# Second layer of batches 2 to 4 in block products with its output transposed, all weights made during batch 1

## The chip, the cores and the metric

The kernel runs on one core of a Trainium2 chip. The metric is the device time of one execution in microseconds; before the change the median of three runs is 2445.89 (2444.21 to 2447.18). The engines are PE (matrix products), DVE (vector), ACT (scalar activation), POOL (the general engine) and SP (here it issues the DMAs). Each engine works through its own instructions in a fixed order and stops where one of them has to wait.

## What is computed

Masked attention over four batches of eight heads, and a mixture of eight experts on its result, in which every token goes through every expert:

```python
    mask = q_assign[:, :, :, None] == k_assign[:, :, None, :]
    scores = np.where(mask, scale * np.matmul(q, k.transpose(0, 1, 3, 2)), -1000000000.0)
    ...
    for e in range(E):
        h = np.maximum(x @ w1[e], 0.0)
        ye = h @ w2[e]
        out += P[:, e:e + 1] * ye
```

x is 3072 x 512 (four batches of 768 tokens), w1 is 8 x 512 x 1024, w2 is 8 x 1024 x 512, all float32. P comes from eight rounds of normalising rows and columns (`gates`). Each operand of a product is held as two float16 numbers, a high part and the remainder, and each product is three matmuls: high by high, high by low, low by high.

## The kernel before

The attention takes the first 530 us. A planner orders its instructions by costs and due times written in the code; it also starts the first weight loads. The change touches one line of it: `largest` (line 290), the largest absolute value of a batch's x, is taken there for the first two batches.

Then come the experts. For every batch, expert and quarter f2 of the hidden size (256 of 1024) there is one step, 128 in all. In a step, layer 1 (`layer1`, with `product`, line 1219) forms four blocks of the hidden values by seven block products in place of eight, from sums of blocks of x (T1 to T4, made once a batch) and of blocks of w1 (S1 to S4, made for each weight). A product is six matmuls of 384 columns; PSUM tiles h_ps (two buffers) receive them, ACT takes m1 and c11 out (line 1252), DVE adds up u2, u3, c22, c21 and c12 (line 1247). ACT writes the high part hh of each block (line 1232), DVE the low part hl (line 1235). Layer 2 (`layer2`, lines 1287 to 1289) multiplies hh and hl as the stationary operand with wb, which holds w2 as high and low part: six token tiles, each six matmuls of 512 columns, into six PSUM tiles o_ps that collect over the four steps of an expert. DVE multiplies by the gate and adds to acc (`gated`, line 1307). The seven products of a step alternate with the six tiles of the step before it.

Batches are taken in pairs, (1, 2) and then (3, 4), and a pair goes through an expert before the next one begins. While the first pair runs, `make_w` makes the 32 weights, one in every two steps in the main: scale the raw weight (ACT, lines 1092 and 1103), four sums of w1 blocks (POOL, line 1101), high parts (ACT) and low parts (POOL, lines 1107, 1110, 1115). They are kept for the pair's first batch, stored to memory (`store_w`) and loaded again (`load_w`) for the others. `scan` loads every raw weight once more ahead of that, to find the largest value of an expert, which sets its scale. `next_x` prepares the x of a later batch. `plan.keep_order` at the end of each seventh of a step fixes the order of everything written so far.

## Time and profile before

| | |
|---|---|
| median of three runs | 2445.89 us |
| span of the profiled execution | 2448.7 us |
| attention, up to the first expert matmul | 532.4 us |
| experts, first matmul to last | 532.4 to 2444.3 us |
| DMA, mean over the span | 131 GB/s |

The profile page holds the span, the busy time of each engine, the chain of work that ended last and the costliest groups of instructions. A row of the timeline begins with start and duration in microseconds, then engine, line, operation, the tiles written and read, and in square brackets the idle time ahead of it and what ended it. A row of the groups ends with total busy time, the mean of one in nanoseconds, and the idle time ahead of the group. PE rows count pipelined matmuls: the distance between starts, and not the duration, is what one costs. PEld is the load of the stationary operand.

### The profile page before, as it was taken

The numbers are of one execution on the slowest core, as the hardware profiler recorded it, in microseconds if no ns is written. First come the engines' busy times: TensorE is split into PE (matmuls) and PEld (weight loads), VectorE is DVE, ScalarE is ACT, GpSimd is POOL, SyncE is SP. The second block draws the span as 40 slices with busy tenths as digits, with TensorE's granted clock in tenths as the row PEclk, the third lists the DMA queues.
The fourth block names the chain that finished last, engine by engine and source line by source line (L and its number), as shares of the span: only waits on it lengthen the run. The fifth ranks groups of instructions, "written<-read, shape, count | busy, mean of one in ns | idle before, by whom it ended". The sixth has DMA issues, their size and how long they took to land.

```text
span 2448.7 us, 32683 instructions
## 1 busy us (share of the span) xinstructions
PE 2383.3 (97%) x12848; PEld 1275.6 (52%) x12848; DVE 1342.4 (55%) x2354; ACT 836.1 (34%) x1616; POOL 672.4 (27%) x712
## 2 busy tenths in 40 slices
...
GB/s 145 119 101 121 102 150 152 84 125 155 164 220 218 146 196 133 212 142 186 171 156 129 127 135 145 95 113 99 95 95 96 111 102 95 95 95 109 104 104 90
DMA packets 154681, 320.29 MB, mean 131 GB/s; under 512 B 61088, under 2 KB 90528, under 8 KB 154016
## 3 DMA queue, kind: packets, MB, share of 16 engines
...
q14 instruction: 52, 0.43, 0.1%
...
## 4 chain that ended last, share of the span: by engine, by line
PE 86%; DVE 7%; issue 3%; ACT 2%; DMA 1%; POOL 0%; SPq 0%; POOLq 0%; ACTq 0%; DVEq 0%
PE h_ps L1219 34%; PE o_ps L1289 13%; PE o_ps L1287 13%; PE o_ps L1288 13%; PE av_ps L824 4%; PE max_ps L697 3%; PE exp_ps L765 2%; DVE mrt L701 2%; PE exp_ps L766 2%; DVE vsum L507 1%; PE misc_ps L557 1%; DVE hl L1235 1%; PE misc_ps L861 0%; ACT pe L772 0%; PE misc_ps L940 0%
## 5 line engine op out<-in xcount | busy, mean ns | idle before, releaser
L1219 PEld LDWEIGHTS <-wa 128*128 128x128 f16 x5376 | 528.1, 98 | 451.7 <-issue 26.9
L1219 PE MATMUL h_ps<-xsT,wa 128*128 128x384 f16 x3072 | 585.1, 327 | 9.2 <-DVE csum L1055 7.8
L1289 PE MATMUL o_ps<-wb,hl 128*128 128x512 f16 x1536 | 583.2, 380 | 1.4 <-DVE hl L1235 1.4
L1232 ACT ACTIVATE hh<-c 128x384 f16<-128x384 f32 x512 | 267.5, 523 | 927.7 <-DVE c L1247 916.6
L1288 PE MATMUL o_ps<-wb,hh 128*128 128x512 f16 x1536 | 583.1, 380 | 0.0
L1287 PE MATMUL o_ps<-wb,hh 128*128 128x512 f16 x1536 | 583.0, 380 | 0.0
L1235 DVE SCALAR_TENSOR_TENSOR hl<-c,hh 128x384 f16<-128x384 f32 x512 | 291.0, 568 | 493.1 <-ACT hh L1232 492.6
L1219 PE MATMUL h_ps<-xsB,wa 128*128 128x384 f16 x2304 | 421.4, 328 | 7.4 <-DVE c L1247 7.4
L1247 DVE SCALAR_TENSOR_TENSOR c<-h_ps,u 128x384 f32<-128x384 f32 x256 | 142.2, 555 | 193.1 <-PE h_ps L1219 193.0
L1289 PEld LDWEIGHTS <-hl 128*128 128x128 f16 x1536 | 150.5, 98 | 184.6 <-DVE hl L1235 3.4
L1247 DVE SCALAR_TENSOR_TENSOR u<-h_ps,m 128x384 f32<-128x384 f32 x256 | 142.3, 556 | 182.6 <-PE h_ps L1219 182.5
L791 POOL TENSOR_TENSOR psum<-psum,pe 128x512 f32<-128x512 f32 (+1 forms) x207 | 227.2, 1115 | 54.2 <-ACT pe L772 46.6
L1287 PEld LDWEIGHTS <-hh 128*128 128x128 f16 x1536 | 151.0, 98 | 139.2 <-issue 0.6
L1288 PEld LDWEIGHTS <-hh 128*128 128x128 f16 x1536 | 150.4, 98 | 139.6 <-issue 0.6
L701 DVE TENSOR_REDUCE mrt<-max_ps 128x1 f32<-128x512 f32 (+1 forms) x288 | 190.5, 683 | 46.3 <-PE max_ps L697 44.6
L1252 ACT ACTIVATE c<-h_ps 128x384 f32<-128x384 f32 x128 | 62.7, 490 | 424.7 <-PE h_ps L1219 424.7
L772 ACT ACTIVATE pe<-exp_ps 128x512 f32<-128x512 f32 x288 | 166.5, 597 | 88.8 <-PE exp_ps L766 82.6
L1101 POOL TENSOR_TENSOR r<-r 128x256 f32<-128x256 f32 x124 | 88.3, 733 | 372.4 <-ACT r L1092 370.0
L1307 DVE SCALAR_TENSOR_TENSOR acc<-o_ps,gates,acc 128x512 f32<-128x512 f32 x168 | 125.4, 747 | 41.3 <-PE o_ps L1289 41.1
L824 PE MATMUL av_ps<-pe,vn 128*64 128x512 f32 (+1 forms) x768 | 138.5, 504 | 0.0
L697 PE MATMUL max_ps<-kX,qX 96*128 96x256 f32 (+1 forms) x384 | 126.9, 393 | 5.5 <-DVE mrt L701 2.6
L766 PE MATMUL exp_ps<-qX,kX 98*128 98x512 f32 (+1 forms) x384 | 128.5, 347 | 0.0
...
## 6 DMA issues: line engine op xcount, KB each, us to landing
...
```

The costliest lines, as they stand in the source:

```text
L697: nc.tensor.matmul(ps[:, y * (z - a) : (y + 1) * (z - a)], t["qa"][0:96, i * P : (i + 1) * P], t["k2"][0:96, a:z], start=True, stop=True)
L701: nc.vector.tensor_reduce(out=t["mr"][:, i0 : i0 + ni, ni - 1], in_=ps.rearrange("p (x c) -> p x c", x=ni), axis=AX, op=ALU.max)
L766: nc.tensor.matmul(o, t["k2"][0:98, ki], t["qa"][0:98, a:z], start=False, stop=True)
L791: (nc.gpsimd if e == POOL else nc.vector).tensor_tensor(out=st[:, a:z], in0=old[a], in1=part, op=ALU.add)
L824: nc.tensor.matmul(av[o, a:z], vn[:, i, :], heads[t]["pe", c][:, i - i0], start=(i == 0), stop=False, skip_group_check=True)
L1219: nc.tensor.matmul(ps[:, 0:HB], wa[:, w_, a, c, :], x[:, x_, c, :], start=(first and s_ == 0), stop=(s_ == len(steps) - 1), skip_group_che ...
L1232: nc.scalar.activation(hh[:, 2 - i, o], src, AF.Relu)
L1235: nc.vector.scalar_tensor_tensor(out=hl[:, 2 - i, o], in0=src, scalar=0.0, in1=hh[:, 2 - i, o], op0=ALU.max, op1=ALU.subtract)
L1247: nc.vector.scalar_tensor_tensor(out=t, in0=ps[:, 0:HB], scalar=KAPPA, in1=x, op0=ALU.mult, op1=ALU.add)
L1287: nc.tensor.matmul(po[i], hh[:, t, ti], wbh[:, t], start=(first and t == 0), stop=False)
L1288: nc.tensor.matmul(po[i], hh[:, t, ti], wbl[:, t], start=False, stop=False)
L1289: nc.tensor.matmul(po[i], hl[:, t, ti], wbh[:, t], start=False, stop=(last and t == 1))
```

## The change

The first batch alone now runs through all eight experts and makes every weight (phase 1, 32 steps). Raw weights are loaded once, six steps ahead, into seven tiles; the largest values are taken from these tiles (`scan`). One weight is made in each step, with two additions: `second_matrix` makes the low part of wb on DVE in place of POOL, and `second_sums` forms four sums of w2 blocks (POOL) with their high (ACT) and low parts (DVE), tile w2s. Its own layer 2 is as before.

Batches 2 to 4 follow (phase 2) in 24 slots of batch and expert, 28 steps each. A step holds one product of layer 1 of this slot and one group of six matmuls of layer 2 of the slot before, all of 384 columns. Layer 2 now has seven block products too (`layer2b`): a stored block of w2 or of its sums (w2o) is stationary, the hidden blocks ho are moving, so the output comes out transposed. The hidden blocks stay in float32 (B11 to B22) and their differences T1 to T4 are formed by `minus`, on POOL but for T1 and T2 of the second half (g = 1), which are DVE's; `high` (ACT) and `low` (DVE) split them. The gate, now a row over tokens, is multiplied and added on POOL (`gated_block`); at the last expert `deliver` turns the block back by six transposes of PE and stores it. x of the next batch is prepared by `next_x` in the first batch and in the second slot of a batch, stored, and loaded again (`reload_x`). The attention takes `largest` for the first batch only.

```diff
-            if b < 2:
+            if b == 0:
...
-    order = [(2 * c + j, e) for c in range(B // 2) for e in range(E) for j in range(2)]
...
-    def begin(idx):
-
-        e, j = divmod(idx, NP2)
-        return j - 1 if e == 0 else 2 * NP2 + j - 1 if e == 1 else 2 * NP2 * e + 2 * j - NP2 - 1
-
-    made = {}
-    begins = {begin(i): i for i in range(NI)}
-    scan_at = {1: NP2 - 1, 2: 2 * NP2 - 1, **{e: 2 * NP2 * (e - 1) - NP2 - 1 for e in range(3, E)}}
...
-            if b == 0:
-                store_w(idx, wt)
-            if t in begins:
-                i = begins[t]
-                made[i] = w_tiles(True)
-                making = make_w(i, made[i])
-                if i + 1 < NI:
-                    load_raw(i + 1)
-            for x, t0 in scan_at.items():
-                if t0 == t:
-                    scanning = scan(x)
...
+        def second_matrix(idx, wb):
+            e = idx // NP2
+            r2 = raws[idx][:, 1024:2048].rearrange("p (j m) -> p j m", j=2)
+            nc.scalar.activation(wb[:, 0], r2, AF.Copy, scale=s2[:, e : e + 1])
+            nc.vector.scalar_tensor_tensor(out=wb[:, 1], in0=r2, scalar=s2[:, e : e + 1], in1=wb[:, 0], op0=ALU.mult, op1=ALU.subtract)
+
+        def second_sums(idx):
+            e = idx // NP2
+            r2 = raws[idx][:, 1024:2048].rearrange("p (j m) -> p j m", j=2)
+            S_ = sump.tile([P, 4, HD], F32, name="s2w")
+            sums(S_, r2[:, 1, 0:HD], r2[:, 0, 0:HD], r2[:, 1, HD:DO], r2[:, 0, HD:DO], nc.gpsimd)
+            yield
+            t = w2s[idx] = w2p.tile([P, 4, 2, HD], F16, name="w2s")
+            nc.scalar.activation(t[:, :, 0], S_, AF.Copy, scale=s2[:, e : e + 1])
+            nc.vector.scalar_tensor_tensor(out=t[:, :, 1], in0=S_, scalar=s2[:, e : e + 1], in1=t[:, :, 0], op0=ALU.mult, op1=ALU.subtract)
+            yield
...
+        def make_w(idx, wt):
+
+            e = idx // NP2
+            wa, wb = wt
+            raw, A, S_ = first_matrix(idx)
+            nc.scalar.activation(raw, raw, AF.Copy, scale=s1[:, e : e + 1])
+            sums(S_, A[:, 1, 0], A[:, 1, 1], A[:, 0, 0], A[:, 0, 1], nc.gpsimd)
+            yield
+            for o, a in ((A22, A[:, 0, 1]), (slice(A11, A12 + 1), A[:, 1])):
+                nc.scalar.copy(wa[:, 0, o], a)
+                nc.gpsimd.tensor_tensor(out=wa[:, 1, o], in0=a, in1=wa[:, 0, o], op=ALU.subtract)
+            yield
+            nc.scalar.copy(wa[:, 0, 3:7], S_)
+            nc.gpsimd.tensor_tensor(out=wa[:, 1, 3:7], in0=S_, in1=wa[:, 0, 3:7], op=ALU.subtract)
+            yield
+            second_matrix(idx, wb)
+            yield
+            yield from second_sums(idx)
...
+        def store_sums(idx):
+            e, f2 = divmod(idx, NP2)
+            nc.sync.dma_start(out=w2d[e][:, 3:7, f2], in_=w2s.pop(idx))
...
+        scans = {1: (4, 5), 2: (6, 7), **{i - 5: (i,) for i in range(8, NI)}}
...
+        for t in range(NI):
...
+            if t + AHEAD < NI:
+                load_raw(t + AHEAD)
+            if t + 1 < NI:
+                wts[t + 1] = w_tiles()
+                making = chain(making, make_w(t + 1, wts[t + 1]))
...
+            if t in scans:
+                scanning = chain(*(scan(i) for i in scans[t]))
+            if t == 8:
+                inputs = next_x(1)
...
+            for m, _ in enumerate(layer1(wt[0], xs[0], out_tile, keep)):
                 if m in (0, 1, 3, 4):
                     step(sink)
-                if m in (((6,), (0, 3, 6), ANY, ANY)[t - NP2 + 1] if NP2 - 1 <= t < 2 * NP2 - 1 else (0, 2, 3, 5) if t < 11 else (0, 3)):
+                if m in ANY:
                     step(scanning)
...
                 step(before)
                 step(making)
+                if m == 1:
+                    store_w(t, wt)
+                    store_sums(t)
+                if t == NI - 1:
+                    reload_x(1, RIGHT[m])
                 plan.keep_order()
...
+    slots = [(b, e) for b in range(1, B) for e in range(E)]
...
+    def minus(n, g, o, a, c, into, by):
+        d = blocks[n, g]
+        t = d[into] if into else hbp.tile([P, 2, HB], F32, name="T3", bufs=2)
+        by.tensor_tensor(out=t, in0=d[a], in1=d[c], op=ALU.subtract)
+        d[o] = t
+
+    def high(n, g, o):
+        t = halves_[n, g, o] = hop.tile([P, 2, 2, HB], F16, name="ho")
+        nc.scalar.copy(t[:, 0], blocks[n, g][o])
+
+    def low(n, g, o):
+        t = halves_[n, g, o]
+        nc.vector.tensor_tensor(out=t[:, 1], in0=blocks[n, g][o], in1=t[:, 0], op=ALU.subtract)
...
+    def plan_slot(n):
+
+        base = SLOT * (n + 1)
+        for g, (t3, t1, t2, t4), off in ((0, (-13, -12, -4, 4), -6), (1, (1, 2, 3, 5), -4)):
+            at(base + t3, minus, n, g, "T3", "B22", "B12", None, nc.gpsimd)
+            at(base + t1, minus, n, g, "T1", "B12", "B11", "B12", nc.vector if g else nc.gpsimd)
+            at(base + t2, minus, n, g, "T2", "B22", "T1", "B11", nc.vector if g else nc.gpsimd)
+            at(base + t4, minus, n, g, "T4", "B21", "T2", "B21", nc.gpsimd)
+            for i, (_, o) in enumerate(ORDER2):
+                at(base + 4 * i + off, high, n, g, o)
+                at(base + 4 * i + off + 1, low, n, g, o)
+        for i in range(7):
+            at(base + 4 * i - 8, load_left, n, i)
+        at(base - 8, load_gate, n)
...
+                for d in range(2):
+                    nc.tensor.transpose(
+                        out=ps[:, ((q - q0) * 2 + d) * P : ((q - q0) * 2 + d + 1) * P], in_=y[:, d, q * P : (q + 1) * P], identity=ident
+                    )
...
+            nc.gpsimd.tensor_tensor(out=a, in0=y, in1=G_, op=ALU.mult)
+            return
+        nc.gpsimd.tensor_tensor(out=y, in0=y, in1=G_, op=ALU.mult)
+        to = y if e == E - 1 else a
+        nc.gpsimd.tensor_tensor(out=to, in0=y, in1=a, op=ALU.add)
+        if e == E - 1:
+            at(time, deliver, n, r, j, y)
...
+    def layer2b(n):
+
+        base = SLOT * (n + 1)
+        pa, pb, pc, y = {}, {}, {}, {}
...
+        for i, (a, o) in enumerate(ORDER2):
+            for d in range(2):
+                ps, pl, name, first = ((pa, ps_a, "pa", i == 0), (pb, ps_b, "pb", i == 2), (pc, ps_c, "pc", i == 4))[(0, 0, 1, 1, 2, 1, 2)[i]]
+                if first:
+                    ps[d] = pl.tile([P, 512], F32, name=name)
+                ps = ps[d]
+                for g in range(2):
...
+                    for s_, (w_, h_, f) in enumerate(steps):
+                        nc.tensor.matmul(
+                            ps[:, 0:HB],
+                            w[:, 2 * g + f, w_, d * P : (d + 1) * P],
+                            h[:, h_, f],
+                            start=(first and g == 0 and s_ == 0),
+                            stop=(g == 1 and s_ == len(steps) - 1),
...
+                    if g == 1:
+                        if i in (1, 4, 5, 6) and d == 0:
+                            y[i] = yp.tile([P, 2, HB], F32, name="y")
+                        if i == 0:
+                            nc.scalar.copy(mt[:, d], ps[:, 0:HB])
+                        elif i == 1:
+                            nc.scalar.copy(y[i][:, d], ps[:, 0:HB])
+                        elif i == 2:
+                            plus(u2[:, d], mt[:, d], ps)
+                        elif i == 3:
+                            plus(u3[:, d], mt[:, d], ps)
+                        else:
+                            plus(y[i][:, d], (u3, mt, u2)[i - 4][:, d], ps)
+                        if d == 1 and i in (1, 4, 5, 6):
+                            r, j = {1: (0, 0), 4: (1, 1), 5: (1, 0), 6: (0, 1)}[i]
+                            gated_block(n, r, j, y[i], base + {1: 11, 4: 22, 5: 25, 6: SLOT + 9}[i])
+                    yield
...
+            def keep(name, c):
+                if name == "B11":
+                    nc.scalar.activation(out_tile(name), c[:, 0:HB], AF.Relu, scale=KAPPA)
+                else:
+                    rests.append(lambda: nc.scalar.activation(c, c, AF.Relu))
+
+            for m, _ in enumerate(layer1(wa, xs[b], out_tile, keep)):
+                if e == E - 1 and f2 == NP2 - 1 and b + 1 < B:
+                    reload_x(b + 1, RIGHT[m])
+                yield
+
...
+    for n in range(NS + 1):
+        one = layer1b(n) if n < NS else iter(())
+        two = layer2b(n - 1) if n else iter(())
+        if n < NS:
+            b, e = slots[n]
+            if e == 1 and b + 1 < B:
+                inputs = next_x(b + 1)
+            if e == E - 1 and b + 1 < B:
+                inputs = spread_gates(b + 1)
+        for s in range(SLOT):
...
+            step(one)
+            for f in old:
+                f()
+            for f, a in tasks.pop(now, ()):
+                f(*a)
+            if s % 7 == 5:
+                step(inputs)
+            step(two)
+            plan.keep_order()
```

The first place is ACT in the middle of the weight making. Before, a step that makes a weight holds these rows (r1 and r2 are the raw halves, c11 and the others the blocks of the hidden values):

```order
L1092 ACTIVATE r1_13106<-r1_13106,s1_96 128x1024 [waits DMAHW6_49]
L1103 ACTIVATE r2_13108<-r2_13108,s2_97 128x1024 [waits DMAHW7_49]
L1252 ACTIVATE c11_13398<-h_ps_13356 128x384 [waits PE_49,Activation_49]
L1232 ACTIVATE hh_13354<-c11_13398 128x384 [waits Activation_49]
L1106 CAST wa_13348<-r1_13106 128x256
L1106 CAST wa_13348<-r1_13106 128x512
L1109 CAST wa_13348<-r1_13106 128x1024 [waits Pool_49]
L1232 ACTIVATE hh_13354<-c22_13435 128x384 [waits DVE_49]
L1232 ACTIVATE hh_13354<-c21_13451 128x384 [waits DVE_49]
L1232 ACTIVATE hh_13354<-c12_13467 128x384 [waits DVE_49]
L1114 CAST wb_13349<-r2_13108 128x1024
L1252 ACTIVATE m1_13486<-h_ps_13479 128x384 [waits PE_49]
```

After, these rows of phase 1 run from the second-layer sums of one weight to those of the next (raw is the raw weight, c the blocks):

```order
L1238 ACTIVATE w2s_8111<-s2w_8089,s2_97 128x4x256 [waits DMAHW6_49,Pool_49]
L1373 ACTIVATE hh_7988<-c_8120 128x384 [waits DVE_49]
L1147 ACTIVATE m1_8140<-h_ps_8133 128x384 [waits PE_49]
L1268 ACTIVATE raw_7384<-raw_7384,s1_96 128x1024
L1272 CAST wa_8129<-raw_7384 128x256 [waits DMAHW2_49,Activation_49]
L1272 CAST wa_8129<-raw_7384 128x512
L1370 ACTIVATE c_8187<-h_ps_8133 128x384 [waits PE_49]
L1373 ACTIVATE hh_8131<-c_8187 128x384 [waits Activation_49]
L1275 CAST wa_8129<-s1w_8150 128x1024 [waits Pool_49]
L1228 ACTIVATE wb_8130<-raw_7384,s2_97 128x1024 [waits DMAHW5_49,DMAHW4_49,DMAHW3_49]
L1373 ACTIVATE hh_8131<-c_8225 128x384 [waits DVE_49]
L1373 ACTIVATE hh_8131<-c_8247 128x384 [waits DVE_49]
```

The high part w2s of the sums, which waits for POOL, stands ahead of the last hh of the step, of m1 and of the scaling of the next raw weight.

The second place is POOL in the same two stretches. Before, one weight is:

```order
L1101 TENSOR_TENSOR r1_11089<-r1_11089 128x256 [waits DMAHW2_49,Activation_49]
L1101 TENSOR_TENSOR r1_11089<-r1_11089 128x256 [waits Pool_49]
L1101 TENSOR_TENSOR r1_11089<-r1_11089 128x256
L1101 TENSOR_TENSOR r1_11089<-r1_11089 128x256 [waits Pool_49]
L1107 TENSOR_TENSOR wa_11343<-r1_11089,wa_11343 128x256 [waits DMAHW6_49,PE_49,Activation_49]
L1107 TENSOR_TENSOR wa_11343<-r1_11089,wa_11343 128x512 [waits Activation_49]
L1110 TENSOR_TENSOR wa_11343<-r1_11089,wa_11343 128x1024 [waits Activation_49]
L1115 TENSOR_TENSOR wb_11344<-r2_11091,wb_11344 128x1024 [waits DMAHW7_49,PE_49,Activation_49]
```

After, one weight is:

```order
L1219 TENSOR_TENSOR s1w_8150<-raw_7384 128x256 [waits DMAHW7_49,Activation_49]
L1219 TENSOR_TENSOR s1w_8150<-s1w_8150,raw_7384 128x256 [waits Pool_49]
L1219 TENSOR_TENSOR s1w_8150<-raw_7384 128x256
L1219 TENSOR_TENSOR s1w_8150<-raw_7384,s1w_8150 128x256 [waits Pool_49]
L1273 TENSOR_TENSOR wa_8129<-raw_7384,wa_8129 128x256 [waits DMAHW2_49,PE_49,Activation_49]
L1273 TENSOR_TENSOR wa_8129<-raw_7384,wa_8129 128x512 [waits Activation_49]
L1276 TENSOR_TENSOR wa_8129<-s1w_8150,wa_8129 128x1024 [waits Activation_49]
L1219 TENSOR_TENSOR s2w_8236<-raw_7384 128x256 [waits DVE_49]
L1219 TENSOR_TENSOR s2w_8236<-s2w_8236,raw_7384 128x256 [waits Pool_49]
L1219 TENSOR_TENSOR s2w_8236<-raw_7384 128x256
L1219 TENSOR_TENSOR s2w_8236<-raw_7384,s2w_8236 128x256 [waits Pool_49]
```

Four sums s2w have come, and the low part of wb has gone to DVE; the first s1w row waits for ACT's scaling.

The third place is DVE in phase 2, at the beginning of a slot, which has no counterpart before (B12, B11 and so on are hidden blocks, y and u2o outputs of layer 2):

```order
L1443 TENSOR_TENSOR ho_12454<-B21_12056,ho_12454 128x768 [waits Activation_49]
L1504 TENSOR_TENSOR y_12444<-pc_12304,u2o_11967 128x384 [waits PE_49]
L1138 SCALAR_TENSOR_TENSOR u2_12517<-h_ps_12510,m1_12493 128x384 [waits PE_49,Activation_49]
L1443 TENSOR_TENSOR ho_12496<-B21_12317,ho_12496 128x768 [waits Activation_49]
L1434 TENSOR_TENSOR B12_12340<-B12_12340,B11_12262 128x768 [waits Pool_49]
L1138 SCALAR_TENSOR_TENSOR u3_12553<-h_ps_12510,m1_12493 128x384 [waits PE_49]
L1443 TENSOR_TENSOR ho_12537<-B11_12001,ho_12537 128x768 [waits Activation_49]
L1434 TENSOR_TENSOR B11_12262<-B22_12300,B12_12340 128x768 [waits DVE_49]
L1138 SCALAR_TENSOR_TENSOR B22_12571<-h_ps_12564,u3_12553 128x384 [waits DVE_49,PE_49]
L1138 SCALAR_TENSOR_TENSOR B21_12590<-h_ps_12510,m1_12493 128x384 [waits PE_49]
L1443 TENSOR_TENSOR ho_12574<-B11_12262,ho_12574 128x768 [waits Activation_49]
```

The difference of the second half, written over B12, waits for POOL, and u3 and B22 of layer 1 stand behind it. On POOL these rows belong to it:

```order
L1491 TENSOR_TENSOR y_12374<-y_12374,gate_11818 128x768 [waits DVE_49]
L1493 TENSOR_TENSOR acc_11156<-y_12374,acc_11156 128x768 [waits Pool_49]
L1434 TENSOR_TENSOR B11_12001<-B22_12037,B12_12076 128x768 [waits Activation_49]
L1491 TENSOR_TENSOR y_12444<-y_12444,gate_11818 128x768 [waits DVE_49]
L1493 TENSOR_TENSOR acc_11156<-y_12444,acc_11156 128x768 [waits Pool_49]
L1434 TENSOR_TENSOR T3_12519<-B22_12300,B12_12340 128x768 [waits Activation_49]
L1434 TENSOR_TENSOR B21_12056<-B21_12056,B11_12001 128x768
```

T3 of the second half stands behind the two rows of each gated block and T2 of the first half.

515 lines of the change are left out of this document (275 added, 240 removed).

## Prediction

> **What bounds the kernel now.** I read the page first (engines, then the chain of waits), then the windows, then the timeline of PE.
>
> ```profile
> span 2448.7 us, 32683 instructions
> PE 2383.3 (97%) x12848; PEld 1275.6 (52%) x12848; DVE 1342.4 (55%) x2354; ACT 836.1 (34%) x1616; POOL 672.4 (27%) x712
> PE 86%; DVE 7%; issue 3%; ACT 2%; DMA 1%; POOL 0%; SPq 0%; POOLq 0%; ACTq 0%; DVEq 0%
> ```
>
> The chain is 86% PE, so the time is made of matmuls. The windows say where this holds; their columns are the busy times of PE, PEld, DVE, ACT and POOL with instruction counts, then clock, DMA share and GB/s.
>
> ```profile
> 532.40:560.00 27.60, 21.45 (x90) 10.74 (x90) 18.07 (x40) 12.48 (x19) 15.84 (x14) 0.72 0.54 193
> 560.00:620.00 60.00, 50.62 (x262) 25.84 (x261) 44.73 (x78) 21.44 (x35) 21.27 (x14) 0.97 0.36 138
> 680.00:740.00 60.00, 55.73 (x289) 28.41 (x288) 30.53 (x54) 26.37 (x42) 29.42 (x26) 0.97 0.62 226
> 740.00:857.00 117.00, 117.00 (x628) 61.19 (x627) 58.26 (x103) 42.52 (x72) 35.62 (x32) 1.00 0.47 172
> 1557.00:2141.00 584.00, 583.28 (x3119) 304.82 (x3117) 243.44 (x433) 119.50 (x242) 0.00 (x0) 1.00 0.27 100
> ```
>
> From 740 on PE is never idle, at full clock, while POOL, which makes weights, is busy 30% (35.6 of 117) and later not at all. In 532 to 740 PE does stop. One step (42 layer-1 and 36 layer-2 matmuls) is read from the starts:
>
> ```profile
> 1588.86 2.11 PE L1219 MATMUL h_ps<-xsB,wa 128*128 128x384 f16 x12
> 1590.81 0.38 PE L1287 MATMUL o_ps<-wb,hh 128*128 128x512 f16 x1
> 1591.03 0.38 PE L1288 MATMUL o_ps<-wb,hh 128*128 128x512 f16 x1
> 1603.46 0.81 PE L1219 MATMUL h_ps<-xsB,wa 128*128 128x384 f16 x4
> ```
>
> Twelve matmuls of 384 columns take 1590.81 - 1588.86 = 1.95 us, 0.1622 each. The whole step is 1603.46 - 1588.86 = 14.60, so the 36 of 512 columns share 14.60 - 6.81: 0.2162 each, as their starts show.
>
> **The column term.** Layer 2 took 3456 matmuls (96 steps x 36) of 0.2162, 747.2 us. Afterwards it has 24 slots x 28 steps x 6 = 4032 of 0.1622, 654.0 us. That is **-93.2**, if PE stays fed.
>
> **Phase 1, the weight loop.** Batch 0 now makes a whole weight in every step of 14.6; before, one took two steps. The work per weight also grows: four POOL sums for W2, an ACT cast and a DVE subtract of them. In the order listings these engines hang together in a ring, which needs durations:
>
> ```profile
> 780.55 2.90 POOL L1101 TENSOR_TENSOR r<-r 128x256 f32<-128x256 f32 x4 [12.95 <-ACT r L1092]
> 784.93 1.87 POOL L1107 TENSOR_TENSOR wa<-r,wa 128x256 f16<-128x256 f32 x2 [1.48 <-ACT wa L1106]
> 786.76 2.12 POOL L1110 TENSOR_TENSOR wa<-r,wa 128x1024 f16<-128x1024 f32 x1
> L1092 ACT ACTIVATE r<-r,s 128x1024 f32<-128x1024 f32 x31 | 35.3, 1138 | 0.0
> L1232 ACT ACTIVATE hh<-c 128x384 f16<-128x384 f32 x512 | 267.5, 523 | 927.7 <-DVE c L1247 916.6
> L1252 ACT ACTIVATE m<-h_ps 128x384 f32<-128x384 f32 x128 | 60.7, 475 | 2.1 <-PE h_ps L1219 2.1
> L1247 DVE SCALAR_TENSOR_TENSOR c<-h_ps,u 128x384 f32<-128x384 f32 x256 | 142.2, 555 | 193.1 <-PE h_ps L1219 193.0
> 1485.73 1.02 DVE L307 SCALAR_TENSOR_TENSOR xsT<-tx,sx,xsT 128x768 f16<-128x768 f32 x1 [1.42 <-ACT xsT L304]
> ```
>
> POOL's share is 2.90 (W1 sums) + 1.87 + 2.12 + 2.90 (W2 sums, the same shape) = 9.8. The casts it needs fit inside the sums. Behind the last W2 sum come, one after another: ACT w2s 1.14, DVE w2s (1024 elements; 1.02 x 1024/768 = 1.36), DVE c12 0.56, ACT hh 0.52, ACT m1 0.48, ACT scale of the next raw weight 1.14, and only then POOL's next sum. With 0.2 for five hand-overs this is 5.4, so the ring turns in **15.2**, call it 15.3, against PE's 14.6. PE pays at the second product of each step, which waits for c12. What is queued behind the waiting ACT w2s is hh, m1 and the scale, which is why the ring closes.
>
> Then DVE and POOL hinder each other, as two places show:
>
> ```profile
> 693.13 3.22 POOL L1101 TENSOR_TENSOR r<-r 128x256 f32<-128x256 f32 x4
> 694.39 0.70 DVE L1235 SCALAR_TENSOR_TENSOR hl<-c,hh 128x384 f16<-128x384 f32 x1 [1.05 <-ACT hh L1232]
> 698.06 2.12 POOL L1110 TENSOR_TENSOR wa<-r,wa 128x1024 f16<-128x1024 f32 x1
> 698.71 1.89 DVE L1235 SCALAR_TENSOR_TENSOR hl<-c,hh 128x384 f16<-128x384 f32 x1 [0.59 <-ACT hh L1232]
> 1486.88 2.00 POOL L300 TENSOR_TENSOR tx<-xqB,tx 128x768 f32<-128x768 f32 x1 [32.88 <-issue]
> 1487.13 2.56 DVE L307 SCALAR_TENSOR_TENSOR xsB<-xqB,sx,xsB 128x768 f16<-128x768 f32 x1
> 1488.96 2.40 POOL L300 TENSOR_TENSOR tx<-xqB,xqB 128x768 f32<-128x768 f32 x1
> 1490.22 1.14 PE L1219 MATMUL h_ps<-xsT,wa 128*128 128x384 f16 x6 [0.73 <-DVE u L1247]
> ```
>
> The hl at 698.71 takes 1.89 instead of 0.56: it ends 0.4 after the POOL subtract that was running. The hl inside the four sums lengthens them from 2.90 to 3.22. The 1.02 us subtract takes 2.56 beside POOL, the POOL operation behind it 2.40 instead of 2.00, and PE then stands 0.73. The page "SBUF — State Buffer" of the Trainium skill, section "Who interferes with whom", gives the rule: the one port pair that VectorE and GpSimd share is an exclusive lock, and the section "SBUF: two separate sides" puts a VectorE operation with two SBUF inputs among those that take it, for the whole instruction. By that rule the sums of the two operations add up wherever they meet, which speaks against this change; the rows agree (1.89 against 0.56, 3.22 against 2.90).
>
> In the new loop POOL works without a break for 9.8 us. Three hl and the wb subtract (1024 elements, now DVE's) become ready inside that stretch. Price: 3 x 0.32 from the first pair of rows, and about 0.8 for wb, since 0.40 was lost behind one of 768 elements and the subtract itself is 1.36. Sum 1.7, with 0 and 3.0 (all four added whole: 3 x 0.56 + 1.36) as its ends; I take 1.7, nearest to the rows. Period 17.0: +2.4 over 29 steps (the first and the last two aside), **+69.6** (ends +20 and +107).
>
> Phase 1 moves per step a raw weight (1.05 MB) and the stores of one weight (0.92 for w1, 0.92 for w2 and its sums): 2.9 MB in 14.6 us, 199 GB/s, under the 226 of the window at 680; cost 0.
>
> **Each new expert.** The scale now waits for the reduction of its weights, on the same ring:
>
> ```profile
> 808.86 0.13 DVE L246 TENSOR_SCALAR gm<-gm 2x1 f32<-2x1 f32 x1
> 809.21 0.22 DVE L249 TENSOR_SCALAR gd<-ident,gm 2x2 f32<-2x2 f32 x1
> ```
>
> Three such operations take 0.57; three more and a matmul between them make some 1.4 (an estimate). Seven experts: **+9.8** (0 to 14).
>
> **The start.**
>
> ```profile
> 550.05 2.08 PE L1219 MATMUL h_ps<-xsB,wa 128*128 128x384 f16 x6 [4.73 <-DVE c L1247]
> 553.02 0.63 PE L1289 MATMUL o_ps<-wb,hl 128*128 128x512 f16 x1
> 553.44 0.63 PE L1287 MATMUL o_ps<-wb,hh 128*128 128x512 f16 x1
> ```
>
> PE already waits 4.73 there. Now the first raw weight is loaded after the last small attention transfers instead of before them, and the second weight follows it through the same engines: **+6** (0 to 12). The two windows 560 to 620 and 680 to 740 hold 262 and 289 instructions where 60 us at the full rate (628 in 117) hold 322: 11.2 and 6.2 us lost, to the doubled work of two interleaved batches and to scan loads. These go: **-17.4** (0 to -25, if the slack of the window before 560 goes too).
>
> **Phase 2, slots of 54.5 us.** Per slot DVE has some 28 PSUM operations of 0.56, 14 subtracts of 768 elements at about 1.0 and two more: 32 us. POOL has 14 operations of about 1.9, 27 us. Each fits. But the DVE subtract T1 of the second half waits for POOL's T3, queued behind two POOL operations of the gate, at the slot's start; behind it on DVE stand u3 and c22, which PE needs. A layer-1 buffer has 2 x 1.95 - 0.97 - 0.56 = 2.4 us of slack, POOL's queue is 2 to 4 us long. Price 0 to 2; I take 1.0, a little over the 0.73 that PE lost at 1490.22: **+24** (0 to +48). DMAs: a slot loads four wa (0.92 MB each), seven w2o (0.52) and a gate (0.39), 7.7 MB in 54.5 us or 142 GB/s, where the window at 740 bore 172 with PE never idle; cost 0. The attention part loses one reduction:
>
> ```profile
> L290 DVE TENSOR_REDUCE amx<-xT 128x1 f32<-128x3072 f32 x2 | 6.7, 3353 | 0.1
> ```
>
> It is 3.35 us of DVE in a part whose planner reorders what follows: 0 (between -3 and +3).
>
> **Output side.** Batches 1 to 3 need 72 fp32 transposes.
>
> ```profile
> L872 PEld LDWEIGHTS misc_ps<-ident,sc x48: 137/140/223, 81.2 to 520.8; 128*128 128x128 f32 x48
> 2443.90 0.38 PE L1289 MATMUL o_ps<-wb,hl 128*128 128x512 f16 x1
> 2444.32 0.75 DVE L1307 SCALAR_TENSOR_TENSOR acc<-o_ps,gates,acc 128x512 f32<-128x512 f32 x1 [0.54 <-PE o_ps L1289]
> ```
>
> At 0.137 apart: **+9.9** (up to +15 if they wait for the gate). The last matmul ends at 2444.28, 4.4 us ahead of the span's end; now an add (0.56), two gate operations (2.0 each by the POOL rows), transposes and a copy (0.5 each) and the store (3.6, the 4.4 less the add) stand there, 9.2. That is +4.8, and the last slot, which has no layer 1 beside it, gets +2: **+7** (4 to 12).
>
> **Sum**: -93.2 + 69.6 + 9.8 + 6 - 17.4 + 24 + 9.9 + 7 = **+15.7** on 2448.7, 2464.4. The median of the runs, 2445.9, lies 2.8 below that execution: **2461**.
>
> **Rivals.** *A: POOL does not pay.* If the DVE operations fall into POOL's gap, or POOL's dispatch hides them, the ring is 15.3 and the term 20 instead of 70: **2412**, faster. For it: the steady window 740 to 857 shows POOL means at their plain durations. Against: there POOL works 30% of the time, here 60%. It decides at a period of 16.5, where the sum is zero; the price of conflicts must stay under 1.2 a step. *B: the clock drops.* In phase 1 the stall at a new expert is 2.4 + 1.4 = 3.8 us. After the stall of 4.73 the matmuls of 512 columns start 0.43 apart instead of 0.216 until 554.7, about 2.3 us lost; seven times that is +16, **2478**. After the 0.73 at 1490.22 nothing of the kind is seen, so a stall of 2.4 alone should not do it. The page "TensorE: Matmul & The Clock Gate" of the Trainium skill, Part 1, lets the clock halve after an idle window of about 3.4 us, which would include the 3.8. *C: phase 2 starves.* If three DVE subtracts per slot meet POOL late, at 0.73 each, the term is 53 instead of 24: **2490**. For it: POOL and DVE then hold their shared path 27 + 16 of 54.5 us. Against: subtracts fall on every second step, and the next one catches up.
>
> **How the numbers follow.** Forecast 0.47 (2435 to 2480), A 0.30, B 0.13, C 0.10. 8 in 10 is 2405 to 2495: it takes in A down to 2405 and C. What a measurement of this kernel can tell from no change is about 0.2%, 5 us: faster 0.33 (A without its upper edge, and the forecast's lower edge), same 0.12, slower 0.55.
>
> **What would show it.** Between 560 and 1080 the changed profile should show steps of 17.0 with one PE stall of about 2.4 on DVE's c; POOL busy 60 to 70%; ACT's w2s ended by POOL. From there, twelve matmuls in 1.95 us with a stall at each slot's start. If phase 1's steps are 15.3 or less, A holds and I am wrong in sign; if PE stands in phase 2's middle, C.

## The result, and the profile after

The changed kernel takes 2484.76 us (median of four runs, 2484.17 to 2486.93), the kernel before 2446.53 beside it: a ratio of 1.0153 with an interval of 1.0138 to 1.0168. It is slower, as forecast, but by 38 us and not by 15. The profiled execution has a span of 2482.9, 34.2 more than the one before.

The first lines of the page and the chain of waits, in the form of those shown of before:

```profile
span 2482.9 us, 35511 instructions
PE 2325.9 (94%) x13499; PEld 1341.5 (54%) x13499; DVE 1749.4 (70%) x2506; ACT 1094.1 (44%) x1972; POOL 1388.9 (56%) x1133
PE 59%; DVE 17%; POOL 12%; issue 5%; ACT 4%; DMA 2%; SPq 1%; ACTq 0%; DVEq 0%; POOLq 0%
```

PE is busy for 57 us less, and yet the end comes later. Of the chain, 27 points have gone from PE to the others, 12 of them to POOL, which held none of it. The windows (PE, PEld, DVE, ACT, POOL, then clock, DMA share, GB/s) say where:

```profile
560.00:590.00 30.00, 21.45 (x105) 10.48 (x103) 27.05 (x47) 10.56 (x16) 13.76 (x14) 0.89 0.42 143
830.00:860.00 30.00, 28.14 (x150) 14.79 (x151) 22.10 (x30) 15.60 (x23) 18.55 (x20) 1.00 0.39 128
860.00:890.00 30.00, 24.58 (x122) 12.01 (x121) 19.66 (x32) 12.95 (x20) 15.38 (x16) 0.94 0.43 133
1500.00:1800.00 300.00, 292.57 (x1799) 175.95 (x1798) 199.85 (x260) 122.22 (x215) 146.37 (x73) 1.00 0.49 161
2430.00:2483.00 53.00, 32.57 (x186) 18.72 (x184) 22.55 (x23) 12.77 (x22) 25.50 (x13) 0.89 0.26 79
```

Phase 1 holds 150 instructions of PE in an ordinary 30 us and 122 where a new expert begins; full rate is 161. Phase 2 keeps PE at 97.5%. The last 53 us stand out: 32.6 of PE.

The length of a step in phase 1 is the distance between the first layer-2 matmul of each:

```profile
547.60 0.59 PE L1301 MATMUL o_ps<-wb,hh 128*128 128x512 f16 x1
...
1097.16 0.38 PE L1301 MATMUL o_ps<-wb,hh 128*128 128x512 f16 x1
```

549.6 us for 31 steps, 97.1 more than 31 of 14.595. One by one: the first two take 46.4, the six in which experts 3 to 8 begin take 132.2 (22.0 each), the other 23 take 371.0 (16.1 each). An ordinary step and the beginning of an expert, as rows of POOL, DVE and PE:

```profile
646.83 0.73 POOL L1219 TENSOR_TENSOR s1w<-raw 128x256 f32<-128x256 f32 x1 [5.02 <-ACT raw L1268]
651.02 0.15 DVE L1210 TENSOR_REDUCE am<-am 128x2 f32<-128x8 f32 x1
651.76 2.13 POOL L1276 TENSOR_TENSOR wa<-s1w,wa 128x1024 f16<-128x1024 f32 x1
651.90 3.06 DVE L1229 SCALAR_TENSOR_TENSOR wb<-raw,s,wb 128x1024 f16<-128x1024 f32 x1 [0.73 <-ACT wb L1228]
653.84 1.70 POOL L1219 TENSOR_TENSOR s2w<-raw 128x256 f32<-128x256 f32 x1
656.68 0.55 DVE L1138 SCALAR_TENSOR_TENSOR c<-h_ps,m 128x384 f32<-128x384 f32 x1
657.28 0.27 PE L242 MATMUL h_ps<-ident,am 128*2 128x128 f32 x1 [2.23 <-DVE c L1138]
661.53 0.38 PE L252 MATMUL h_ps<-gd,ones 2*128 2x2 f32 x2 [1.71 <-DVE gd L249]
663.97 0.63 PE L1302 MATMUL o_ps<-wb,hh 128*128 128x512 f16 x1
664.39 0.63 PE L1303 MATMUL o_ps<-wb,hl 128*128 128x512 f16 x1
665.39 0.73 POOL L1219 TENSOR_TENSOR s1w<-raw 128x256 f32<-128x256 f32 x1 [7.36 <-ACT raw L1268]
```

POOL stands 5.02 us for ACT's scaling, the hand-over of the forecast (5.4). The wb subtract, 1.3 us of work, takes 3.06 because POOL's 2.13 us subtract is running, and POOL's next sum takes 1.70 instead of 0.73. At the new expert PE meets the two passes of the scale and stands 2.23 and 1.71 us. The input of the first pass, am, was ready at 651.17; the pass starts at 657.28, when DVE has read c out of a PSUM tile h_ps, of which there are two and which the passes share with layer 1. The second pass waits for its own input, gd. The next matmuls are 0.42 apart, half speed; m1 of the next step, which the scaling waits behind, is late by that, and POOL's gap grows to 7.36. The page "TensorE: Matmul & The Clock Gate" of the Trainium skill, Part 1, puts the drop after an idle window of about 3.4 us; here neither stall is that long, and the clock fell.

### The profile page after: what moved, and what is told of

Its sections match the earlier page's. It is cut to its first block, busy times and chain, and to the rows that moved or that the text cites. A ratio compares the mean times of both kernels' runs of the same rounds, so it can differ in the third digit from the quotient of the medians.

```text
span 2482.9 us, 35511 instructions
## 1 busy us (share of the span) xinstructions
PE 2325.9 (94%) x13499; PEld 1341.5 (54%) x13499; DVE 1749.4 (70%) x2506; ACT 1094.1 (44%) x1972; POOL 1388.9 (56%) x1133
## 4 chain that ended last, share of the span: by engine, by line
PE 59%; DVE 17%; POOL 12%; issue 5%; ACT 4%; DMA 2%; SPq 1%; ACTq 0%; DVEq 0%; POOLq 0%
PE h_ps L1124 23%; PE pb L1516 11%; PE pc L1516 6%; PE av_ps L824 4%; PE pa L1516 3%; DVE B L1434 3%; PE max_ps L697 3%; PE exp_ps L765 2%; POOL y L1491 2%; POOL s2w L1219 2%; POOL T L1434 2%; PE exp_ps L766 2%; DVE mrt L701 2%; POOL acc L1493 1%; DVE w2s L1239 1%
## 5 line engine op out<-in xcount | busy, mean ns | idle before, releaser
L1516 PEld LDWEIGHTS <-w2o 128*128 128x128 f16 x4032 | 395.1, 98 | 265.6 <-issue 8.0
L1443 DVE TENSOR_TENSOR ho<-B,ho 128x768 f16<-128x768 f32 x288 | 370.9, 1288 | 1.0 <-ACT ho L1439 0.9
L1516 PE MATMUL pb<-ho,w2o 128*128 128x384 f16 x1728 | 329.1, 327 | 4.8 <-DVE ho L1443 4.2
L1439 ACT CAST ho<-B 128x768 f16<-128x768 f32 x288 | 234.8, 824 | 89.1 <-DVE B L1434 87.2
L1434 POOL TENSOR_TENSOR B<-B,B 128x768 f32<-128x768 f32 x96 | 205.0, 2135 | 82.2 <-DVE B L1434 72.3
L791 POOL TENSOR_TENSOR psum<-psum,pe 128x512 f32<-128x512 f32 (+1 forms) x203 | 222.2, 1112 | 44.4 <-ACT pe L772 40.3
L1516 PE MATMUL pa<-ho,w2o 128*128 128x384 f16 x1152 | 218.4, 327 | 0.0
L1516 PE MATMUL pc<-ho,w2o 128*128 128x384 f16 x1152 | 217.8, 326 | 0.0
L1373 ACT ACTIVATE hh<-c 128x384 f16<-128x384 f32 x128 | 66.9, 523 | 232.4 <-DVE c L1138 217.2
L1493 POOL TENSOR_TENSOR acc<-y,acc 128x768 f32<-128x768 f32 x72 | 154.7, 2149 | 5.6
L1303 PE MATMUL o_ps<-wb,hl 128*128 128x512 f16 x384 | 150.2, 391 | 6.7 <-DVE hl L1376 6.6
```

The source lines that it names most:

```text
L791: (nc.gpsimd if e == POOL else nc.vector).tensor_tensor(out=st[:, a:z], in0=old[a], in1=part, op=ALU.add)
L1303: nc.tensor.matmul(po[i], hl[:, t, ti], wbh[:, t], start=False, stop=(last and t == 1))
L1434: by.tensor_tensor(out=t, in0=d[a], in1=d[c], op=ALU.subtract)
L1439: nc.scalar.copy(t[:, 0], blocks[n, g][o])
L1443: nc.vector.tensor_tensor(out=t[:, 1], in0=blocks[n, g][o], in1=t[:, 0], op=ALU.subtract)
L1493: nc.gpsimd.tensor_tensor(out=to, in0=y, in1=a, op=ALU.add)
```

## The experiments

All are edits of the changed kernel. In the table the step times are taken as above, from one profiled execution each (the ordinary step is the mean of 23, among them those in which the next batch's x is prepared); "phase 2" runs from the start of the first layer-2 matmul of phase 2 to the end of the last, "ratio" is against the kernel before, with its interval.

| kernel | median us | ratio | ordinary step | new expert's step | phase 2 |
|---|---|---|---|---|---|
| changed | 2484.8 | 1.0153 [1.0138, 1.0168] | 16.13 | 22.0 | 1339.7 |
| e1 sums later | 2495.1 | 1.0205 [1.0180, 1.0229] | 16.64 | 21.9 | 1338.1 |
| e2 one scale | 2467.4 | 1.0085 [1.0068, 1.0103] | 16.57 | 17.6 | 1340.0 |
| e3 T3 on DVE | 2470.4 | 1.0095 [1.0078, 1.0112] | 16.12 | 22.2 | 1321.8 |
| e4 last gate on DVE | 2481.6 | 1.0142 [1.0125, 1.0159] | 16.26 | 22.1 | 1335.1 |
| e5 scale spread | 2475.6 | 1.0116 [1.0092, 1.0141] | 16.10 | 19.3 | 1342.4 |
| e6 wb low zero | 2452.3 | 1.0026 [1.0012, 1.0039] | 15.11 | 19.9 | 1339.7 |
| e7 e3, e4, e5 | 2442.3 | 0.9989 [0.9975, 1.0003] | 16.03 | 19.5 | 1314.2 |
| e8 scale early | 2472.1 | 1.0108 [1.0085, 1.0130] | 15.86 | 20.0 | 1339.7 |
| e9 wb behind sums | 2492.3 | 1.0181 [1.0164, 1.0198] | 16.29 | 22.2 | 1339.8 |
| e10 low in four | 2498.8 | 1.0210 [1.0190, 1.0230] | 16.25 | 22.8 | 1339.7 |
| e11 e7 and e8 | 2434.2 | 0.9949 [0.9934, 0.9964] | 16.00 | 18.5 | 1314.2 |
| e12 e11 and e9 | 2465.9 | 1.0076 [1.0061, 1.0091] | 16.75 | 19.8 | 1313.9 |

### What sets an ordinary step of phase 1

e6 leaves out the low part of wb: its place is written with zeros by ACT.

```diff
-            nc.vector.scalar_tensor_tensor(out=wb[:, 1], in0=r2, scalar=s2[:, e : e + 1], in1=wb[:, 0], op0=ALU.mult, op1=ALU.subtract)
+            nc.scalar.activation(wb[:, 1], r2, AF.Copy, scale=0.0)
```

> The low part of wb is left out: ACT writes zeros in place of DVE's subtract with two inputs. DVE loses 1.3 us of work a step, POOL none, ACT gains about 1.1. Theory (the subtract waits for POOL, 3.06 us where it works 1.28, holds DVE's sums for PE meanwhile, and makes POOL's next sum 1.70 instead of 0.73): ordinary steps fall from 16.1 to 15.2 or less, the time by 20 to 35 us. Rival (the ring sets the step and wb stands outside it): 5 us or less.

32 us less, inside the theory's 20 to 35, and the ordinary step falls to 15.11. The group of POOL's first and third W2 sum shows what else went: first the changed kernel, with its two DVE subtracts, then e6.

```profile
L1219 POOL TENSOR_TENSOR s2w<-raw 128x256 f32<-128x256 f32 x64 | 84.2, 1315 | 10.7 <-ACT m L1147 10.7
L1229 DVE SCALAR_TENSOR_TENSOR wb<-raw,s,wb 128x1024 f16<-128x1024 f32 x32 | 79.5, 2483 | 11.2 <-ACT wb L1228 10.9 <-DMA raw<-in_moe_w 0.4
L1239 DVE SCALAR_TENSOR_TENSOR w2s<-s2w,s,w2s 128x1024 f16<-128x1024 f32 x32 | 41.7, 1302 | 11.4 <-ACT w2s L1238 11.3
```

```profile
L1219 POOL TENSOR_TENSOR s2w<-raw 128x256 f32<-128x256 f32 x64 | 47.1, 735 | 10.7 <-DMA raw<-in_moe_w 10.7
```

The same 64 sums take 84.2 us beside the subtract and 47.1 without it: POOL lost 1.16 us in each of 32 weights, and DVE 1.18 (2.48 for work that takes 1.30). e6 also takes 1.3 us of DVE's work away. POOL's beat, the distance between the first W1 sums of two weights, tells the two apart. In the last steps, which no new expert and no x of the next batch disturb, it is, in the changed kernel and in e6:

```profile
1053.45 0.73 POOL L1219 TENSOR_TENSOR s1w<-raw 128x256 f32<-128x256 f32 x1 [5.38 <-ACT raw L1268]
1069.68 0.73 POOL L1219 TENSOR_TENSOR s1w<-raw 128x256 f32<-128x256 f32 x1 [5.02 <-ACT raw L1268]
```

```profile
1015.69 0.73 POOL L1219 TENSOR_TENSOR s1w<-raw 128x256 f32<-128x256 f32 x1 [5.02 <-ACT raw L1268]
1030.83 0.73 POOL L1219 TENSOR_TENSOR s1w<-raw 128x256 f32<-128x256 f32 x1 [5.02 <-ACT raw L1268]
```

The beat is 16.23 us, of which 5.02 is the hand-over and 11.21 POOL's work; in e6 it is 15.14, with the same hand-over and 10.12 of work. The hand-over, where DVE's part of the ring lies, did not change, so the 1.1 us are POOL's own, lost in the meeting. The ring without the meeting of wb was forecast at 15.3 and is 15.1.

e1 moves the split of the W2 sums (w2s, ACT and DVE) into the next step, so that it no longer stands between POOL's last sum and the next weight's scaling:

```diff
-                    store_sums(t)
+                if m == 2:
+                    split_sums(t)
+                if m == 4:
+                    store_sums(t)
```

> The high and low parts of the W2 sums are made in the next step, after its scaling, so that nothing of ACT's or DVE's stands between POOL's last sum and the next weight's scaling. Theory (the ring of POOL, ACT w2s, DVE w2s, c12, hh, m1 and scale sets phase 1's step): ordinary steps fall from 16.1 us to 14.6 to 15.0, the time by 30 to 50 us, to 2435 to 2455. Rival (the shared use of the port and DVE's load set it, wherever the sums are split): the time falls by less than 10 us.

This expectation of the ring theory failed: 10 us more. The groups of e1:

```profile
L1244 DVE SCALAR_TENSOR_TENSOR w2s<-s2w,s,w2s 128x1024 f16<-128x1024 f32 x32 | 82.8, 2588 | 34.1 <-ACT w2s L1243 29.0 <-POOL wa L1277 3.4 <-issue 1.7
L1229 DVE SCALAR_TENSOR_TENSOR wb<-raw,s,wb 128x1024 f16<-128x1024 f32 x32 | 42.4, 1324 | 0.4 <-ACT wb L1228 0.4
L1219 POOL TENSOR_TENSOR s2w<-s2w,raw 128x256 f32<-128x256 f32 x32 | 40.9, 1278 | 2.5
L1219 POOL TENSOR_TENSOR s1w<-raw 128x256 f32<-128x256 f32 x62 | 45.4, 732 | 178.9 <-ACT raw L1272 178.9
```

In its old place w2s ran in POOL's gap, at 1.30. Now it meets POOL's subtract and takes 2.59, wb behind it 1.32, and the second W2 sum pays (1.28 instead of 0.76). Nor is the ring open: hh and m1 still stand ahead of the scaling on ACT, and POOL waits for the scaling for 178.9 us in all, where it waits for 185.4 in the changed kernel (its row stands under e8). The edit moved DVE's operation to the place where POOL is busy and gained next to nothing in the hand-over.

e8 takes the scaling out of the hand-over: ACT scales the next raw weight two sevenths before the step's end.

```diff
+                if m == 4 and t + 2 < NI and (t + 2) % NP2:
+                    scale_raw(t + 2)
```

> ACT scales the next raw weight two sevenths before the end of the step instead of behind w2s, hh and m1 (not at a new expert's first weight), so POOL goes from the last W2 sum straight to the next W1 sums. Theory (the ring's hand-over sets the step): 20 to 35 us less. Rival, after the sums made later brought 10 us more (a DVE subtract of 1024 elements that meets POOL at work costs as much as the gap it closes): the w2s subtract now meets POOL's W1 sums, and the time changes by less than 10 us either way.

13 us less by the medians, between the two expectations. The ordinary step gains only 0.27; the steps of new experts gain 2.0 each. POOL's waits, first in the changed kernel, then in e8:

```profile
L1219 POOL TENSOR_TENSOR s1w<-raw 128x256 f32<-128x256 f32 x62 | 45.7, 737 | 185.4 <-ACT raw L1268 185.4
L1276 POOL TENSOR_TENSOR wa<-s1w,wa 128x1024 f16<-128x1024 f32 x31 | 66.1, 2132 | 14.9 <-ACT wa L1275 14.9
```

```profile
L1219 POOL TENSOR_TENSOR s1w<-raw 128x256 f32<-128x256 f32 x62 | 61.9, 998 | 62.5 <-ACT raw L1265 62.5
L1281 POOL TENSOR_TENSOR wa<-s1w,wa 128x1024 f16<-128x1024 f32 x31 | 67.3, 2170 | 73.3 <-ACT wa L1280 73.3
L1278 POOL TENSOR_TENSOR wa<-raw,wa 128x256 f16<-128x256 f32 x31 | 20.8, 669 | 26.1 <-ACT wa L1277 26.1
```

POOL goes on to the W1 sums, and there w2s now meets them (998 ns instead of 737). Then it waits for ACT's casts of wa, which still stand behind m1: 99.4 us where it was 14.9. So e8, like e1, moves the place where the ring closes and does not take it apart; no run here has an open ring.

e9 puts wb behind the W2 sums, e10 cuts POOL's 2.13 us subtract into four.

```diff
-            second_matrix(idx, wb)
-            yield
-            yield from second_sums(idx)
+            rest = second_sums(idx)
+            next(rest)
+            yield
+            second_matrix(idx, wb)
+            yield
+            yield from rest
```

> wb's two parts stand behind the four W2 sums in the order, instead of ahead of them, so DVE's subtract meets POOL's operations of 0.73 us or none, and not the one of 2.13 us. Theory (what counts is how long the POOL operation is that DVE has to sit out): 5 to 15 us less than the changed kernel. Rival (ACT's and DVE's wb now stand in the ring's hand-over and lengthen it): no gain, or up to 40 us more (1.3 in each of 29 steps).

```diff
-            nc.gpsimd.tensor_tensor(out=wa[:, 1, 3:7], in0=S_, in1=wa[:, 0, 3:7], op=ALU.subtract)
+            for o in range(4):
+                nc.gpsimd.tensor_tensor(out=wa[:, 1, 3 + o], in0=S_[:, o], in1=wa[:, 0, 3 + o], op=ALU.subtract)
```

> POOL's subtract of 1024 elements for the low parts of the W1 sums is cut into four of 256 (0.75 us each by the row of one such, 3.0 in place of 2.13). DVE's wb subtract waits for a quarter at most. Theory of the shared port: DVE is held some 1.3 us less, while the ring grows by 0.9; the sum is between 10 us less and 15 us more, and wb's row falls from 3.06 to about 2. If wb's row stays at 3, the port's lock is not what holds it.

Both shorten wb and both lose, 8 and 14 us. In e9 it falls from 2483 to 1590 ns, but POOL's wait for the scaling grows from 185.4 to 205.1 us, which is the rival of that expectation. In e10 wb falls to 1518 ns, and POOL's cut subtract takes 4 x 930:

```profile
L1277 POOL TENSOR_TENSOR wa<-s1w,wa 128x256 f16<-128x256 f32 x124 | 111.8, 930 | 16.0 <-ACT wa L1275 15.9
L1229 DVE SCALAR_TENSOR_TENSOR wb<-raw,s,wb 128x1024 f16<-128x1024 f32 x32 | 48.6, 1518 | 10.7 <-ACT wb L1228 9.5 <-DMA w2d<-wb 1.3
```

The beat of e10 in the same last steps:

```profile
1059.37 0.73 POOL L1219 TENSOR_TENSOR s1w<-raw 128x256 f32<-128x256 f32 x1 [5.02 <-ACT raw L1268]
1076.30 0.73 POOL L1219 TENSOR_TENSOR s1w<-raw 128x256 f32<-128x256 f32 x1 [5.01 <-ACT raw L1268]
```

So the length of the POOL operation that DVE sits out is real, but it does not set the step: what POOL and the hand-over gain in length does. POOL's cut subtract is 3.72 - 2.13 = 1.6 us longer a weight, wb 1.0 shorter; the beat is 16.93, again 5.01 of hand-over and 11.92 of work. In three kernels the beat is POOL's work plus the same 5.0 us, and it moves as POOL's work does. That is the ring, with the meetings as a part of its length.

### New experts

e2 gives experts 2 to 8 the first one's scale, so the largest value of their weights is not used.

```diff
-                yield from weight_scale(e, am2, h_tile, gs)
+                for s_ in (s1, s2, so):
+                    nc.vector.tensor_copy(s_[:, e : e + 1], s_[:, 0:1])
+                yield
```

> Experts 2 to 8 take the scale of the first one, so the largest value of their weights is not used and the two small PE passes and ten small DVE operations of each scale fall away; the reductions stay. Theory (the scale's PE pass stands ahead of the next step's first product and closes the ring longer, and the clock falls behind the stall): the six steps of 21 to 25 us become ordinary ones of 16, the time falls by 35 to 45 us. Rival (the prediction's size, only the small operations themselves): 10 us. Second rival (these steps are long for a load that comes late): no change.

17 us less. The new expert's step falls from 22.0 to 17.6; experts 5 and 7 keep 21.0 and 20.4, in the stretch where the next batch's x is prepared. The ordinary step rises from 16.13 to 16.57 and takes back 10 of the 27 us. So this work costs more than the forecast's 10 us, but less than the 35 of the theory. None of the three cases of the expectation was met.

e5 does the same work with the two PE passes further apart from each other and from their DVE inputs:

```diff
+                if m or f2 < NP2 - 1:
                     yield
...
-                    step(scanning)
+                    step(scanning, 2 if m == 2 and t > 2 and t % NP2 == 2 else 1)
```

> The same scale work, but both reductions of an expert's last quarter stand in the first seventh of the step and the two PE passes follow in the third and sixth, instead of the sixth and the end. Leaving the scales out brought 17 us. Theory (PE stands at the passes since their DVE input is queued late, not since there is too much work): most of that comes without leaving anything out, 10 to 17 us. Rival (it is the amount of work on DVE and PE): less than 4 us.

9 us less by the medians (16 in the six steps of the profiled execution), just short of the 10 to 17 of the theory. PE waits 0.62 and 1.48 at the passes of the expert shown above, where it waited 2.23 and 1.71:

```profile
656.50 0.27 PE L242 MATMUL h_ps<-ident,am 128*2 128x128 f32 x1 [0.62 <-ACT c L1371]
659.89 1.65 DVE L249 TENSOR_SCALAR gd<-ident,gm 2x2 f32<-2x2 f32 x1
664.46 0.54 DVE L1138 SCALAR_TENSOR_TENSOR c<-h_ps,m 128x384 f32<-128x384 f32 x1
665.06 0.38 PE L252 MATMUL h_ps<-gd,ones 2*128 2x2 f32 x2 [1.48 <-DVE c L1138]
```

The theory named only a part of the wait. gd is ready at 661.54, 3.5 us ahead of its pass, and PE still waits, until DVE has read c out of h_ps at 665.00. What is left of the second wait is that for the buffer; a pass with a PSUM tile of its own was not run.

### Phase 2

In the changed kernel a slot begins like this (POOL, DVE, PE):

```profile
1531.12 2.53 POOL L1434 TENSOR_TENSOR T<-B,B 128x768 f32<-128x768 f32 x1
1533.69 2.55 DVE L1434 TENSOR_TENSOR B<-B,B 128x768 f32<-128x768 f32 x1 [1.70 <-POOL T L1434]
1536.16 0.55 DVE L1138 SCALAR_TENSOR_TENSOR u<-h_ps,m 128x384 f32<-128x384 f32 x1
1536.76 1.14 PE L1124 MATMUL h_ps<-xsT,wa 128*128 128x384 f16 x6 [0.58 <-DVE u L1138]
```

It is the wait of the prediction: DVE's T1 waits 1.70 for POOL's T3, then takes 2.55 because POOL starts its next operation, and u3 behind it comes 0.58 too late for PE. e3 makes T3 on DVE:

```diff
-            at(base + t3, minus, n, g, "T3", "B22", "B12", None, nc.gpsimd)
+            at(base + t3, minus, n, g, "T3", "B22", "B12", None, nc.vector if g else nc.gpsimd)
```

> The difference T3 of a slot's second half is made by DVE instead of POOL, so DVE's T1 no longer waits for POOL's queue at the slot's start. Theory: the stalls of PE before the fourth and fifth step of a slot, 0.83 us in a slot, go: the time falls by 12 to 20 us. Rival (DVE is held by the shared port there anyway, and now has 0.95 us more to do): less than 5 us, or a loss.

14 us less, as the theory had it. The first 23 slots of layer 2 are 19.2 us shorter, 0.84 each; the last one is 1.4 longer, since its matmuls run at half speed for longer. The group of T1 and T2, of the changed kernel and of e3:

```profile
L1434 DVE TENSOR_TENSOR B<-B,B 128x768 f32<-128x768 f32 x48 | 84.0, 1749 | 44.8 <-POOL T L1434 44.8
```

```profile
L1434 DVE TENSOR_TENSOR B<-B,B 128x768 f32<-128x768 f32 x48 | 53.5, 1114 | 0.0
```

DVE's 44.8 us of waiting for POOL are gone, and the operations themselves take 0.64 us less each.

The last slot runs from 2428.80 to 2473.19, 44.4 us where 168 matmuls of 0.1622 are 27.3. PE's stalls in it, in the changed kernel:

```profile
2439.68 1.06 PE L1516 MATMUL pb<-ho,w2o 128*128 128x384 f16 x5 [2.75 <-DVE ho L1443]
2443.31 3.68 PE L1516 MATMUL pb<-ho,w2o 128*128 128x384 f16 x11 [1.43 <-DVE ho L1443]
2462.16 0.87 PE L1477 MATMUL pa<-ident,y 128*128 128x128 f32 x6 [3.10 <-POOL y L1493]
2469.39 0.88 PE L1477 MATMUL pa<-ident,y 128*128 128x128 f32 x6 [3.43 <-POOL y L1493]
2477.59 1.22 PE L1477 MATMUL pa<-ident,y 128*128 128x128 f32 x6 [4.41 <-POOL y L1493]
```

The last of these rows belongs to the tail, behind the slot's last product. With no layer 1 beside it, layer 2 runs through its steps in half the time, so the transposes, set so many steps behind the gate, arrive before POOL has gated. e4 lets DVE do the gate in this slot:

```diff
+        by = nc.vector if n == NS - 1 else nc.gpsimd
...
-        nc.gpsimd.tensor_tensor(out=y, in0=y, in1=G_, op=ALU.mult)
+        by.tensor_tensor(out=y, in0=y, in1=G_, op=ALU.mult)
```

(and the add in the same way)

> In the last slot alone the gate's multiply and add run on DVE, 0.95 us each, instead of POOL, 1.8 us each. Theory (the transposes in PE's order wait for POOL there, 3.1, 3.4 and 4.4 us): the time falls by 6 to 10 us. Rival (the last slot is paced by the hidden blocks' splits): no change.

In the profiled execution phase 2 is 4.6 us shorter and the tail 1.4; the medians differ by 3.2, with intervals that overlap, where 6 to 10 were expected. The last three waits become 0.77, 1.75 and 2.73; the first two stay.

### Together

> T3 of the second half on DVE, the scale's passes apart, and the last slot's gate on DVE, together. If the three places are independent the gains add up: 14 + 3 + what the passes bring (10 to 17), 27 to 34 us less than the changed kernel, 2450 to 2458. If they hide one another, clearly less.

e7 is at 2442.3, 42 us less than the changed kernel, where its parts alone bring 27 and 2450 was the best that was expected; it is as fast as the kernel before.

> The three edits that together gave 2442 (T3 on DVE, the scale's passes apart, the last slot's gate on DVE) and the early scaling that gave 12 us alone. Independent: 2428 to 2434. If the early scaling's gain was in the steps of new experts, which the passes' place mends already: 2440 to 2444.

e11 is at 2434.2, 0.9949 of the time before [0.9934, 0.9964], and so the fastest kernel of the study. That is the upper edge of the first case, so 8 of the 13 us that the early scaling brings alone came on top of the other three.

> As the four edits, and wb behind the W2 sums. With the early scaling there is no gap left in POOL's work, so wb meets the next weight's W1 sums of 0.73 us: if short POOL operations are what matters, 5 to 15 us less than the four edits; if any meeting costs the same, no change.

e12 loses 32 us against e11, which neither case allowed for: with the early scaling, putting wb behind the sums lengthens the ordinary step from 16.00 to 16.75 and the new expert's from 18.5 to 19.8. wb itself is shorter (1489 ns instead of 1916), but POOL waits 136 us for ACT's casts of wa instead of 98. That this wait is the whole loss is not shown.

## Why the prediction was right or wrong

The sum, against what the two profiled executions show. Measured values are lengths beyond PE's pace (14.595 for a step of phase 1, 54.5 for a slot):

| term | forecast | measured |
|---|---|---|
| columns | -93.2 | -93.1 |
| phase 1: loop 69.6, experts 9.8, start 6, before's own losses -17.4 | 68.0 | 97.1 - 30.7 - 4.6 = 61.8 |
| slots 24, transposes 9.9 | 33.9 | 41.8, and 1.3 in the first slot |
| last slot | 2.2 | 17.1 |
| tail | 4.8 | 5.3 |
| sum | 15.7 | 34.2 |

The direction came out as forecast, and the ring is there; the size was not right. The step that failed is the price of the last slot, +2 for "no layer 1 beside it", where 17.1 us were measured: 15 of the 18.5 us between the sum and the result. Two more terms were too small, the scale of a new expert and the clock, which the sum put at nothing; that phase 1 is near all the same is luck, since the ring was priced too high. By the forecast's own working the sum is zero at steps of 16.5 us. Ordinary steps take 16.1, so with its other terms the forecast would have said "faster"; the kernel is slower because those terms are larger.

- **Columns**: right; the matmuls of both layers of phase 2 cost 0.1622 us.
- **Phase 1**: the sum is near, its parts are not. The ring is there, with a hand-over of 5.0 us (5.4 was worked out). POOL's work on it is 11.2 where 9.8 was given without meetings, so the meetings cost 1.4 and not 1.7, and 1.1 of it goes with wb (e6). The beat is 16.2 and not 17.0; the 23 ordinary steps, 16.1 on average, lose 35 us instead of the 55 that they were given. The new experts went the other way: 44.6 us in six steps beyond PE's pace, where the forecast gave 2.4 + 1.4 in each. What failed there is pricing the scale by its own small operations (1.4): its PE passes stand in PE's order ahead of the product that the ring needs, one waits for an h_ps tile that DVE has not yet read and the other for gd, queued on DVE behind w2s and c. e5 got part of this back by their place alone. Rival B, the clock, came with it: behind the passes of these six experts matmuls at half speed lose 1.1 to 1.7 us each time, 9.4 in all, and 5.3 in the first two steps. That is of the size that rival B was given (16), though the kernel before has such a stretch at its start too. The first two steps, with the start and the second expert's scale, take 17.2 beyond PE's pace; 6 and 1.4 had been given.
- **Before's losses**: 17.4 were counted as going, and 30.7 were there (from 552.21 to 2444.28, 127 steps and the last layer 2 at PE's pace are 1861.4). The start at 547.6 against 552.2 can't be put down to the change: in the twelve experiments, with the same attention, it lies between 545.2 and 553.2.
- **Slots**: the mechanism was named rightly, e3 shows it, and it cost 0.84 a slot and not 1.0. The rest, some 22 us, was given 9.9, for the transposes; in it are also the transposes' waits for the gate (4 us before the last slot) and PE's waits at the scale of the next x, which the forecast did not have.
- **Last slot**: without layer 1 beside it the waits of layer 2 are open: 2.75 and 1.43 near its start, 3.10 and 3.43 at the transposes, 11.8 us with two smaller ones, and the clock falls (0.89 in that window). e4 and e7, in which DVE gates, shorten the waits at the transposes, and the slot takes 39.8 and 38.2 us instead of 44.4. Rival C, PE that waits for late DVE inputs all through phase 2, did not hold: from 1500 to 1800 PE is at 97.5%.
- **Rival A** didn't hold: it needed steps of 15.3, and POOL does pay. e6 is the kernel without wb's meeting, and its beat is 15.1.

What stays open: what an ordinary step would take with the ring taken apart, since e1 and e8 only move its closing point; what paces the steps of e8; and how far the medians of e7 gain more than e3, e4 and e5 alone (42 us against 27) for a cause of the edits. In the profiled executions of e3, e4 and e5 the experts start 3.2 to 5.6 us later than in the changed kernel, and in e7 1.1, and the last slot of e3 and e5 takes 45.8 and 48.7 us against 44.4, at half speed for longer; neither the start nor e5's last slot is what their edits change.
